# Chunk attention and two feed-forward layers on one core: tile 8's queries and keys in the later tiles' buffer, the last weights loaded in step 0, two buffers for transposed probabilities

## The chip, the cores and the metric

The kernel runs on one core of a Trainium2 chip. The metric is the device time of one execution in microseconds (us), the median over several executions.

## The reference

Queries, keys and values have 8 batches, 8 heads, 576 positions and 64 columns each. Attention is done within chunks of 64 positions; its result, laid out as 4608 tokens by 512 columns, goes through two feed-forward layers (512 to 2048 to 512) with different activations:

```python
scores = scale * np.matmul(q_c, k_c.transpose(0, 1, 2, 4, 3))   # per chunk of 64
scores = scores - np.max(scores, axis=-1, keepdims=True)
attn = np.exp(scores)
attn = attn / (np.sum(attn, axis=-1, keepdims=True) + 1e-09)
out = np.matmul(attn, v_c)
x = out.transpose(0, 2, 1, 3).reshape(B * S, H * D)
h = x @ w_in1;  g = np.maximum(h, 0.0) + alpha * np.minimum(h, 0.0);  y = g @ w_out1
h = y @ w_in2;  g = h - np.tanh(h);  out = g @ w_out2
```

The four weight matrices arrive as 64-bit floats, read as 64-bit words.

## The kernel before, in words

The tokens are cut into 36 tiles of 128 and into 9 blocks of 512 (4 tiles). The kernel runs 18 passes, the plan: first layer one over the 9 blocks, then layer two. A pass has 16 steps, one for each block `f` of 128 of the 2048 inner columns. In a step TensorE makes the up product of block `f` (`up`, line 412, 12 matrix products into a PSUM buffer of which there are two) and the down product of the step two back (`down`, line 471, 12 products); between them ScalarE and VectorE compute the activation (`act_g`, line 426) and split it into a high and a low half (`split_g`, line 449). Every factor is split that way, so each product is three.

A weight block of layer one is loaded as 64-bit words (`load_w`, line 135), turned to 32-bit floats by ScalarE and VectorE (`convert_a`, lines 107 and 108; `convert_b`, lines 118 to 128) and split by ScalarE (line 153) and GpSimd (line 154). This happens in the first pass, beside its 16 steps: `(f, 0)` is the up weight of block `f`, `(f, 1)` the down weight. Each has a memory slot of its own, `w{which}_{f}`, and some slots are used earlier for something else: 12 and 13 for the queries and keys of tiles 4 to 7, 14 and 15 for those of tiles 0 to 3, `(15, 0)` once more for those of tile 8. The list `LATE` (line 517) says in which step the loads of blocks 10 to 15 are placed.

The attention of tiles 0 to 3 is a prologue. That of tile `t` from 4 on is spread over steps of the passes, from its `base[t]` (line 535: 3, 5, 7, 9 for tiles 4 to 7, 12 for tile 8, then every 4 steps). Its parts are the transposes of queries and keys (`att_a_natural`, line 243, on TensorE; `att_a`, line 267, on VectorE at line 272 for tiles loaded in pieces), the scores (`att_s`, line 278, step base), the softmax (`att_e`, `att_n`, base + 1 and + 2), the transpose of the probabilities and its copies into `ptb` (`att_t`, `att_d`, lines 337, 346 and 347, base + 3), the product with the values (`att_v`, line 349, base + 4, and + 5 for tile 7) and the splitting of the result into the block's input (`att_x`, lines 400 and 404, one step on). Transposes on TensorE, scores and value products use one PSUM buffer, `ps_a`. Where a tile's value product falls in the step of another tile's scores, `beside` lets it use the second part of that tile's buffer.

From tile 9 on the queries and keys of one to two tiles (a unit) are loaded in at least 32 small transfers into a buffer of which there is one, `raw` (`begin_unit`, line 213, `some_loads`, line 232). A unit may begin at the step `free`, and its transfers are spread over the steps up to three before its scores. Tiles with `t % 9 == 4` are loaded whole into the same buffer (`load_natural_late`).

All of this is written in the order of the steps; a planner of the framework then orders each engine's queue by its own times, save in the prologue, which is kept as written. Loads and stores are all issued by SyncE. The lines that decide here:

```python
beside[t] = next((u for u in base if base[u] == pv), None)          # line 574
both = banks.get(beside.get(t)) or new_banks("xp")                  # line 352
turn = {4: 2, 5: 2, 6: 6, 7: 6, 8: 10}                              # line 546
at(r, some_loads, -(-32 // max(1, last - free)))                    # line 558
```

Of the kernel before, what the change touches and what calls it, by code (L numbers as in the profile page):

```python
# [9 lines left out]
F32 = mybir.dt.float32  # L10
# [17 lines left out]
def kernel(  # L28
# [23 lines left out]
    P = 128  # L52
    HP = H // 2
# [5 lines left out]
    const = ctx.enter_context(tc.tile_pool(name="const", bufs=1))  # L59
# [16 lines left out]
    zero = const.tile([P, P], F32, name="zero")  # L76
    bias_sb = const.tile([P, 1], F32, name="bias_sb")
    ktc = const.tile([P, 2, HP, 2, D], F32, name="ktc")
    ptb = const.tile([P, 2, HP, 2, 32], F32, name="ptb")


    wsplit = {}
# [1 line left out]
    def slot(f, which, shape, dtype):  # L84
        return wpool.tile(shape, dtype, tag=f"w{which}_{f}", name=f"w{which}_{f}")
# [91 lines left out]
    raws, qts, kts, vts, ps, pts, xps = {}, {}, {}, {}, {}, {}, {}  # L177
# [22 lines left out]
    def load_natural(t, raw):  # L200
        for i in range(2):
            natural_into(raw[:, i], t, i)
        raws[t] = raw[:, 0], raw[:, 1]

    def load_natural_early(t, f):
        load_natural(t, slot(f[0], f[1], [P, 2, H * D], F32))

    def load_natural_late(t):
        load_natural(t, rawp.tile([P, 2, H * D], F32, tag="raw", name="rawn"))
# [29 lines left out]
    def new_banks(name):  # L239

        return ps_a.tile([P, 2, 512], F32, tag="a", name=name)
# [34 lines left out]
    scs, banks, beside = {}, {}, {}  # L276
# [62 lines left out]

    def att_d(t):  # L340

        pt, pn = pts.pop(t), ptb.rearrange("p e h a i -> p (e h) a i")
        for c in range(2):
            for a in range(2):
                o, i = 64 * c + 32 * a, 64 * c + 32 * (1 - a)
                nc.vector.tensor_copy(pn[o:o + 32, :, 1 - a, :], pt[i:i + 32, :, a, :])
                nc.scalar.activation(out=pn[o:o + 32, :, a, :], in_=pt[o:o + 32, :, a, :], func=AF.Copy)

    def att_v(t):

        vt = vts.pop(t)
        both = banks.get(beside.get(t)) or new_banks("xp")
        xp = both[:, :, HP * D:].rearrange("p c (h d) -> p c h d", h=HP)
        for hp in range(HP):
            for e in range(2):
                for c in range(2):
                    r = slice(64 * c, 64 * c + 64)
                    nc.tensor.matmul(
                        out=xp[64 * e:64 * e + 64, c, hp, :],
                        lhsT=vt[r, 2 * hp + e],  # L360
                        rhs=ptb[r, e, hp].rearrange("p a i -> p (a i)"),
                        start=True,
                        stop=True,
                    )
        xps[t] = xp
# [140 lines left out]
    def split_y(j, kk, x):  # L506
# [7 lines left out]
    NPT = NB // P  # L514
    LAG = 2
    SCRATCH = 10
    LATE = [(0, (10, 0)), (0, (10, 1)), (0, (11, 0)), (0, (11, 1)), (0, (14, 0)), (0, (14, 1)), (3, (13, 0)), (3, (13, 1)), (7, (12, 0)), (7, (12, 1)),
            (12, (15, 0)), (12, (15, 1))]

    events = {}  # L520

    def at(step, fn, *args, first=False):
        todo = events.setdefault(max(step, 0), ([], []))
        todo[0 if first else 1].append((fn, args))
# [8 lines left out]
    base = {}  # L533
# [13 lines left out]
    free = 0  # L547
    for unit in units:
        t = unit[0]
        if t % 9 == 4 and t > 9:  # L550
            turn[t] = base[t] - 1
            at(free, load_natural_late, t)
            free = turn[t] + 1
        elif t >= 9:
            last = base[t] - 3
            at(free, begin_unit, t, len(unit))
            for r in range(free, last + 1):
                at(r, some_loads, -(-32 // max(1, last - free)))
            for i, tt in enumerate(unit):
                at(base[t] - 2 + i, att_a, tt)  # L560
            free = base[t] + len(unit) - 2
        else:
            free = 8
        for t in unit:
            s = base[t]
            at(s, att_s, t)
            at(s + 1, att_e, t, first=True)
            at(s + 2, att_n, t)
            at(s + 3, att_t, t, first=True)
            at(s + 3, att_d, t, first=True)  # L570
    for t in range(NPT, NT // P):
        pv = base[t] + (5 if t == 7 else 4)
        if t != 7:
            beside[t] = next((u for u in base if base[u] == pv), None)
        at(pv - 2, load_v, t)
        at(pv, att_v, t)
        at(pv + 1, lambda t: att_x(t, get_x(t // NPT), t % NPT * P), t)
    for t in turn:
        at(turn[t], att_a_natural, t)
    for step, piece in LATE:  # L580
        at(step, load_w, *piece)
# [24 lines left out]
    with tc.manual_schedule():  # L606
        make_identity(nc, ident)
        nc.vector.memset(zero, 0.0)
        nc.vector.memset(bias_sb, TS[1])
        kt = rawp.tile([P, 4, HP, 2, D], F32, tag="raw", name="kt")  # L610
        for t in range(4):
            if t % 2 == 0:
                qt = slot(10, t // 2, [P, 2, HP, 2, D], F32)
            qts[t], kts[t] = qt[:, t % 2], kt[:, t]
        load_natural_early(0, (15, 0))
        load_natural_early(1, (15, 1))
        load_w(0, 0)
        load_natural_early(2, (14, 0))
        load_natural_early(3, (14, 1))
        load_v(0)  # L620
        load_v(1)
        load_w(1, 0)
        load_v(2, (11, 0))
        load_v(3, (11, 1))
        arow = stage.tile([P, 512], F32, tag="st", name="arow")
        nc.sync.dma_start(out=arow[:KF, :P], in_=alpha.rearrange("(f p) -> f p", p=P))
        load_w(2, 0)
        load_w(0, 1)
        load_w(3, 0)
        load_natural_early(4, (13, 0))  # L630
        load_w(1, 1)
        load_w(4, 0)
        load_natural_early(5, (13, 1))
        load_w(2, 1)
        load_w(5, 0)
        load_natural_early(6, (12, 0))
        load_w(3, 1)
        load_natural_early(7, (12, 1))
        for f in range(4, 10):
            if f > 5:  # L640
                load_w(f, 0)
            load_w(f, 1)

        def warm(n, to=None):
            for _ in range(n):
                nc.tensor.matmul(out=dummy if to is None else to, lhsT=zero, rhs=zero, start=True, stop=True)

        dummy = ps_y.tile([P, P], F32, tag="y3", name="dummy")
        first_banks = new_banks("first")
        x0 = get_x(0)  # L650
        scratch.extend(xpool.tile([P, 4, 512], F32, tag=f"x{w}", name=f"scr{w}") for w in "hl")
        warm(7)
        att_a_early(0, 0)
        warm(1)
        att_a_early(0, 1)
        warm(1)
        att_a_early(1, 0)
        att_s_early(0)
        att_a_early(1, 1)
        att_e(0, True)  # L660
        warm(3)
        att_s_early(1)
        att_n(0)
        convert_a((0, 0))
        att_a_early(2, 0)
        att_e(1, True)
        warm(4)
        att_a_early(2, 1)
        convert_b((0, 0), ops=(0, 1))
        att_t_early(0)  # L670
        warm(2)
        att_s_early(2)
        att_n(1)
        convert_b((0, 0), ops=(2,))
        att_a_early(3, 0)
        att_a_early(3, 1)
        att_e(2, True)
        convert_b((0, 0), ops=(3,))
        warm(3)
        att_s_early(3)  # L680
        att_t_early(1)
        att_n(2)
        split_w(0, 0, nc.gpsimd)
        warm(1)
        att_v_early(0)
        att_e(3, True)
        att_t_early(2)
        att_xh(0, x0, 0)
        att_v_early(1)
        convert_a((1, 0))  # L690
        att_n(3, nc.vector)
        att_xl(0, x0, 0)
        more = first_banks[:, 0, 0:P]
        warm(2, more)
        att_xh(1, x0, P)
        att_v_early(2)
        last_a = att_t_early(3)
        att_xl(1, x0, P)
        convert_b((1, 0), ops=(0, 1))
        att_xh(2, x0, 2 * P)  # L700
        att_xl(2, x0, 2 * P)
        att_v_early(3)
        convert_b((1, 0), ops=(2, 3))
        split_w(1, 0, nc.gpsimd)
        hp0 = up(0, x0, NB, slice(0, 2 * P))
        att_x(3, x0, 3 * P)
        at_ps = first_banks[:, 0, 0:KF]
        nc.tensor.transpose(at_ps, arow[:KF, :P], ident[:KF, :KF])
        nc.scalar.activation(out=alpha_sb, in_=at_ps, func=AF.Copy)
        nc.scalar.activation(out=nalpha_sb, in_=at_ps, func=AF.Copy, scale=-1.0)  # L710
        load_natural_early(8, (15, 0))

    queue, late = [], []

# [9 lines left out]
    for j, (layer, t0) in enumerate(plan):  # L724
        x = get_x(j)
        acc = []
        for f in range(KF):
            hp = up(0, x0, NB, slice(2 * P, NB), hp0) if j == f == 0 else up(f, x, NB)
# [53 lines left out]
```

## Time and profile before

| | |
|---|---|
| median of 3 runs (lowest to highest) | 1731.82 us (1729.38 to 1732.12) |
| the profiled execution | 1729.36 us |
| its span in the profile | 1727.6 us |
| TensorE busy, products | 1670.8 us (97%) |
| VectorE, ScalarE, GpSimd busy | 1324.7, 689.5, 352.3 us |
| the first pass over the weights, about | 45 to 181 us of the span |
| layer one after it, about | 181 to 906 us |
| layer two, about | 906 us to the end |

Times are counted from the start of the span. PE is TensorE (PEld its weight loads), DVE VectorE, ACT ScalarE, POOL GpSimd, SPq SyncE's queue. A row of a timeline gives the start, the duration, the engine, the line of the kernel, the operation, what it writes and reads, how many instructions the row merges, and in brackets the idle time before it with what ended it. The granted clock is the share of TensorE's full speed that the chip granted.

### The profile page before, as it was taken

Reading aid. Unit: us, or ns where it says so; the run is one execution under the profiler, and the core shown is the slowest. Engines: PE = TensorE matmul, PEld = TensorE weight load, DVE = VectorE, ACT = ScalarE, POOL = GpSimd, SP = SyncE. Lnnn points to the kernel's source line nnn. Section 1 sums busy time; section 2 is a strip of 40 time slices with the busy share of each in tenths; the row PEclk is TensorE's granted clock in tenths of the full one; section 3 lists DMA queues with packets and bytes.
Section 4 is the critical chain, followed back from the end, with each engine's and each line's share of the span. In section 5 each row is a group of like instructions: output and inputs, shape, how many; then the busy total and the mean of one; then the engine's idle time right before and its main releaser. Section 6 shows DMA issues by size and latency. Waiting matters only on the chain.

```text
span 1727.6 us, 24773 instructions
## 1 busy us (share of the span) xinstructions
PE 1670.8 (97%) x9389; PEld 1360.8 (79%) x9389; DVE 1324.7 (77%) x2163; ACT 689.5 (40%) x1304; POOL 352.3 (20%) x264
## 2 busy tenths in 40 slices
PE   8877999999999999999999999999999999999998
PEld 7665788788887888888888778888888888888886
DVE  7988866778667868684437797978787878888776
ACT  6665422333322424231334444435353434344433
POOL 3663100000000000000243222222222222222221
PEclk9988999999999999999999999999999999999999
DMA  9811404433153514320422010101010101000000
GB/s 245 253 55 43 133 13 105 116 86 98 50 111 67 156 28 135 57 92 1 146 74 74 1 49 1 49 1 49 1 49 1 49 1 49 1 25 1 25 1 25
DMA packets 215591, 108.58 MB, mean 63 GB/s; under 512 B 170912, under 2 KB 187312, under 8 KB 215472
## 3 DMA queue, kind: packets, MB, share of 16 engines
q1 hardware_dynamic: 215472, 107.01, 22.8%
q8 instruction: 73, 1.20, 0.3%
q14 instruction: 46, 0.38, 0.1%
HBM read 79.70 MB, written 27.26 MB: 62 GB/s over the span
## 4 chain that ended last, share of the span: by engine, by line
PE 51%; DVE 21%; ACT 8%; issue 5%; SPq 3%; DMA 3%; POOL 0%; ACTq 0%; DVEq 0%; POOLq 0%
PE y L478 25%; PE hps L420 24%; DVE g L467 4%; DVE g L469 4%; DVE g L468 4%; DVE g L465 3%; SPq L232 3%; ACT ghi L450 2%; ACT sq L460 2%; DVE ktc L464 2%; ACT w L462 2%; DMA rw<-in_moe_w_in_dram 1%; DVE xl L509 1%; ACT th L461 1%; PE sc L287 1%
## 5 line engine op out<-in xcount | busy, mean ns | idle before, releaser
L420 PE MATMUL hps<-xh,w 128*128 128x512 f32 (+1 forms) x2312 | 589.1, 395 | 18.7 <-DVE g L444 6.2
L420 PEld LDWEIGHTS hps<-xh,w 128*128 128x128 f32 x2312 | 431.1, 189 | 118.2 <-DVE g L444 9.5
L450 ACT ACTIVATE ghi<-g 128x512 fp32r<-128x512 f32 x288 | 181.9, 632 | 721.9 <-DVE g L469 447.6
L451 POOL TENSOR_TENSOR glo<-g,ghi 128x512 fp32r<-128x512 f32 x159 | 218.2, 1372 | 610.4 <-ACT ghi L450 576.7
L420 PE MATMUL hps<-xl,w 128*128 128x512 f32 (+1 forms) x1156 | 311.6, 391 | 0.0
L478 PE MATMUL y<-w,ghi 128*128 128x512 f32 x1152 | 294.2, 393 | 8.2 <-ACT ghi L450 3.7
L478 PE MATMUL y<-ghi,w 128*128 128x512 f32 x1152 | 289.9, 392 | 3.2 <-ACT ghi L450 3.2
L478 PEld LDWEIGHTS y<-w,ghi 128*128 128x128 f32 x1152 | 215.1, 189 | 60.1 <-ACT ghi L450 8.6
L478 PEld LDWEIGHTS y<-ghi,w 128*128 128x128 f32 x1152 | 216.9, 189 | 49.7 <-ACT ghi L450 4.1
L420 PEld LDWEIGHTS hps<-xl,w 128*128 128x128 f32 x1156 | 218.1, 189 | 45.6
L464 DVE TENSOR_SCALAR ktc<-sq 128x512 uint32<-128x512 f32 x144 | 136.3, 947 | 135.0 <-ACT sq L460 135.0
L441 DVE TENSOR_SCALAR g<-hps,alpha_sb 128x512 f32<-128x512 f32 x128 | 95.4, 746 | 93.4 <-PE hps L420 90.8
L332 POOL TENSOR_TENSOR p<-p,rd 128x512 f32<-128x512 f32 x35 | 39.0, 1113 | 618.3 <-DVE rd L331 568.3
L478 PE MATMUL y<-w,glo 128*128 128x512 f32 x576 | 159.1, 389 | 0.0
L478 PE MATMUL y<-glo,w 128*128 128x512 f32 x576 | 157.3, 392 | 0.2 <-POOL glo L451 0.2
L451 DVE TENSOR_TENSOR glo<-g,ghi 128x512 fp32r<-128x512 f32 x129 | 97.3, 754 | 68.8 <-ACT ghi L450 68.5
L478 PEld LDWEIGHTS y<-glo,w 128*128 128x128 f32 x576 | 108.4, 189 | 23.1 <-POOL glo L451 0.6
L478 PEld LDWEIGHTS y<-w,glo 128*128 128x128 f32 x576 | 108.3, 188 | 22.8
L469 DVE COPY_PREDICATED g<-ktc,th 128x512 f32<-128x512 uint32 x144 | 122.9, 853 | 4.4
L467 DVE SCALAR_TENSOR_TENSOR g<-w,g 128x512 f32<-128x512 f32 x144 | 106.6, 741 | 0.0
L462 ACT ACTIVATE w<-sq,bias_sb 128x512 f32<-128x512 f32 x144 | 104.5, 726 | 0.0
L468 DVE SCALAR_TENSOR_TENSOR g<-sq,g 128x512 f32<-128x512 f32 x144 | 100.6, 699 | 4.7
(101 smaller groups left out, 1475.4 us busy)
## 6 DMA issues: line engine op xcount, KB each, us to landing
ysc<-yst SPq DMA_DIRECT2D x36, 256.0 KB, 2.5
yraw<-ysc SPq DMA_DIRECT2D x9, 1024.0 KB, 5.5
out_dram<-yst SPq DMA_DIRECT2D x36, 256.0 KB, 2.5
w<-in_moe_w_in_dram SPq DMA_DIRECT2D x16, 512.0 KB, 6.1
w<-in_moe_w_out_dram SPq DMA_DIRECT2D x16, 512.0 KB, 6.3
rw<-in_moe_w_in_dram SPq DMA_DIRECT2D x32, 256.0 KB, 3.2
rw<-in_moe_w_out_dram SPq DMA_DIRECT2D x32, 256.0 KB, 3.2
w<-wm SPq DMA_DIRECT2D x32, 256.0 KB, 2.1
```

The costliest lines, as they stand in the source:

```text
L232: nc.sync.dma_start(out=o, in_=i)
L420: nc.tensor.matmul(out=hp[:, cols], lhsT=w[:, a, m], rhs=x[b][:, kk, cols], start=(kk == 0 and i == 0), stop=(kk == KD - 1 and i == 2),)
L441: nc.vector.tensor_scalar(out=g, in0=hp, scalar1=0.0, scalar2=alpha_sb[:, f:f + 1], op0=ALU.min, op1=ALU.mult)
L450: nc.scalar.activation(out=hi, in_=g, func=AF.Copy)
L451: lo_engine.tensor_tensor(out=lo, in0=g, in1=hi.bitcast(F32), op=ALU.subtract)
L462: nc.scalar.activation(out=w, in_=sq, func=AF.Square, bias=bias_sb)
L464: nc.vector.tensor_scalar(out=mask, in0=sq, scalar1=0.375 ** 2, scalar2=None, op0=ALU.is_ge)
L465: nc.vector.scalar_tensor_tensor(out=g, in0=sq, scalar=cc, in1=hp, op0=ALU.mult, op1=ALU.mult)
L467: nc.vector.scalar_tensor_tensor(out=g, in0=w, scalar=ce, in1=g, op0=ALU.add, op1=ALU.mult)
L468: nc.vector.scalar_tensor_tensor(out=g, in0=sq, scalar=ca, in1=g, op0=ALU.add, op1=ALU.mult)
L469: nc.vector.copy_predicated(g, mask, th)
L478: nc.tensor.matmul(out=acc[t], lhsT=lhsT, rhs=rhs, start=(f == 0 and i == 0), stop=(f == KF - 1 and i == 2))
```

## The change

Tile 8's queries and keys are loaded into `raw`, the buffer of the later tiles, in place of the slot of weight block 15; block 15's two loads move from step 12 to step 0. The units that use `raw` after it may begin at step 11 in place of 8, so that the 32 transfers of tiles 9 and 10 are placed 16 to a step in steps 11 and 12 in place of 7 to a step from step 8. The value product of tile 6 moves from step 11 to step 12, where tile 8's scores are, and uses their PSUM buffer; its values' load and its splitting move by a step with it. `ptb` has two halves, used in turn by even and odd tiles.

```diff
-    ptb = const.tile([P, 2, HP, 2, 32], F32, name="ptb")
+    ptb = const.tile([P, 2, 2, HP, 2, 32], F32, name="ptb")
...
-        pt, pn = pts.pop(t), ptb.rearrange("p e h a i -> p (e h) a i")
+        pt, pn = pts.pop(t), ptb[:, t % 2].rearrange("p e h a i -> p (e h) a i")
...
-                        rhs=ptb[r, e, hp].rearrange("p a i -> p (a i)"),
+                        rhs=ptb[r, t % 2, e, hp].rearrange("p a i -> p (a i)"),
...
-    LATE = [(0, (10, 0)), (0, (10, 1)), (0, (11, 0)), (0, (11, 1)), (0, (14, 0)), (0, (14, 1)), (3, (13, 0)), (3, (13, 1)), (7, (12, 0)), (7, (12, 1)),
-            (12, (15, 0)), (12, (15, 1))]
+    LATE = [(0, (10, 0)), (0, (10, 1)), (0, (11, 0)), (0, (11, 1)), (0, (14, 0)), (0, (14, 1)), (0, (15, 0)), (0, (15, 1)),
+            (3, (13, 0)), (3, (13, 1)), (7, (12, 0)), (7, (12, 1))]
...
-            free = 8
+            free = 11
...
-        pv = base[t] + (5 if t == 7 else 4)
-        if t != 7:
-            beside[t] = next((u for u in base if base[u] == pv), None)
+        pv = base[t] + (5 if 6 <= t <= 7 else 4)
+        beside[t] = next((u for u in base if base[u] == pv), None)
...
-        load_natural_early(8, (15, 0))
+        load_natural_late(8)
```

## Rows read from the trace of the kernel before

**Rows 1.** The page: busy us (share of the span) and instructions of each engine.

```profile
PE 1670.8 (97%) x9389; PEld 1360.8 (79%) x9389; DVE 1324.7 (77%) x2163; ACT 689.5 (40%) x1304; POOL 352.3 (20%) x264
```

**Rows 2.** Busy time by stretch, columns as in the first line.

```profile
core 0: us, PE busy (x) PEld busy (x) DVE busy (x) ACT busy (x) POOL busy (x), PEclk, DMA share, GB/s
...
60.00:130.00 70.00, 55.23 (x296) 41.74 (x295) 65.25 (x91) 46.04 (x85) 45.51 (x27) 0.88 0.41 108
...
143.80:158.70 14.90, 4.02 (x74) 3.06 (x73) 9.77 (x21) 8.59 (x18) 1.04 (x1) 0.65 0.20 54
158.70:173.00 14.30, 13.75 (x81) 10.51 (x82) 14.19 (x21) 7.98 (x15) 9.39 (x7) 0.89 0.28 45
173.00:906.00 733.00, 726.22 (x4788) 593.00 (x4787) 507.26 (x1004) 231.69 (x471) 64.29 (x54) 1.00 0.33 86
906.00:1728.00 822.00, 807.98 (x3527) 659.48 (x3525) 665.80 (x923) 352.18 (x637) 201.10 (x150) 1.00 0.07 24
```

**Rows 3.** Timeline of TensorE from 135 to 175 us.

```profile
135.92 1.98 PE L420 MATMUL hps<-xh,w 128*128 128x512 f32 x8
...
142.74 1.07 PE L478 MATMUL y<-glo,w 128*128 128x512 f32 x4
147.36 0.63 PE L251 MATMUL tr<-ident,w 128*128 128x128 f32 x4 [3.55 <-issue]
148.78 1.11 PE L251 MATMUL tr<-ident,w 128*128 128x128 f32 x4 [0.79 <-DVE qt L253]
150.58 1.13 PE L358 MATMUL xp<-ptb,v 64*64 64x64 f32 x32 [0.69 <-ACT ktc L255]
154.97 1.13 PE L287 MATMUL sc<-ktc,qt 64*64 64x64 f32 x32 [3.27 <-DVE xl L404]
158.69 3.53 PE L420 MATMUL hps<-xh,w 128*128 128x512 f32 x8 [2.59 <-ACT w L153]
...
174.84 0.69 PE L287 MATMUL sc<-ktc,qt 64*64 64x64 f32 x32
```

**Rows 4.** Timeline of VectorE and ScalarE from 146 to 159 us.

```profile
146.58 0.68 DVE L404 TENSOR_TENSOR xl<-sc,xh 128x512 fp32r<-128x512 f32 x1
...
149.93 0.60 ACT L255 ACTIVATE ktc<-tr 128x512 f32<-128x512 f32 x1 [3.50 <-PE tr L251]
...
151.81 1.69 ACT L347 ACTIVATE ptb<-pt 32x256 f32<-32x256 f32 x4 [1.28 <-PE xp L358]
...
154.13 0.67 ACT L107 ACTIVATE wm<-w 128x512 f32<-128x512 f32 x1
...
156.39 0.59 ACT L435 ACTIVATE neg<-hps 128x512 f32<-128x512 f32 x1
...
156.87 0.60 ACT L436 ACTIVATE g<-hps 128x512 f32<-128x512 f32 x1
...
158.01 0.63 ACT L153 ACTIVATE w<-wm 128x512 fp32r<-128x512 f32 x1
```

**Rows 5.** Timeline of SyncE's queue.

```profile
69.69 7.12 SPq L232 DMA_DIRECT2D raw<-in_q_dram  x13
...
149.92 0.37 SPq L91 DMA_DIRECT2D w<-in_moe_w_in_dram  x1
...
162.45 7.74 SPq L232 DMA_DIRECT2D raw<-in_q_dram  x16
```

**Rows 6.** DMA view of 38 to 66 us: packets and bytes.

```profile
DMA packets 10479, 9.40 MB, mean 336 GB/s; under 512 B 6254, under 2 KB 9326, under 8 KB 10477
```

**Rows 7.** DMA issues from 162 to 181 us; the last column is us to landing (median).

```profile
raw<-in_k_dram SPq DMA_DIRECT2D x16, 32.0 KB, 2.1
```

**Rows 8.** Waits of VectorE over the span: us in total, times, longest.

```profile
DVE ktc L272 <- DMA raw<-in_k_dram: 14.4, 7, 5.4
```

**Rows 9.** Timeline of VectorE and GpSimd at 126 and 154 us.

```profile
126.50 1.73 POOL L451 TENSOR_TENSOR glo<-g,ghi 128x512 fp32r<-128x512 f32 x1
...
127.01 1.50 DVE L118 TENSOR_SCALAR wm<-wm 128x512 f32<-128x512 f32 x1
...
154.82 0.43 DVE L118 TENSOR_SCALAR wm<-wm 128x512 f32<-128x512 f32 x1
```

## The prediction

> **What bounds the kernel now.** I read the page's busy shares first, then the busy time by stretch, then the timeline of one stretch. TensorE is busy for nearly the whole span [rows 1], so only time in which it stands still, or runs at its lower clock, can be won. By stretch [rows 2] there is little of that in most places: from 173 to 906 us TensorE is busy 726.2 of 733 us, from 906 us to the end 808.0 of 822. The losses lie in the first block of 512 tokens. From 60 to 130 us it is busy 55.2 of 70 us while VectorE is busy 65.3 of 70: there the VectorE bounds, with the conversion of weights, and the change takes no instruction out of that. The stretch from 143.8 to 158.7 us is another matter: TensorE works 4.0 of 14.9 us, its granted clock is 0.65, VectorE has 5.1 us idle and ScalarE 6.3.
>
> The timeline of TensorE shows what stands in this hole [rows 3]: the last product before it ends at 143.81 us, then come the transposes of tile 8 in two halves, the value product of tile 6 at 150.58, the scores of tile 8 at 154.97, and at 158.69 the up product of weight block 15. The other engines' rows [rows 4] say why each is late. The transposes wait for the low half of tile 5's result (146.58 + 0.68 = 147.26 us), since all of these share one PSUM buffer. The keys of tile 8 are copied out at 149.93 + 0.60 = 150.53. The product of tile 6 then takes the buffer for itself, and the scores get it only when ScalarE and VectorE have read that product: 150.58 to 154.97, 4.4 us. Meanwhile SyncE's load of weight block 15, which reuses the memory of tile 8's queries and keys, is issued at 149.92 us, right after the transposes have read it [rows 5]. ScalarE starts a conversion at 154.13, and only behind the conversions in its queue come the two readings of a finished up product at 156.39 to 157.47; the split at 158.01 releases TensorE. So three things end together near 158.6: the late weights, the late reading of the product's buffer, and the PSUM handoff.
>
> **The change part by part.** *Weights of block 15 at step 0, tile 8 in the later tiles' buffer.* The wait of the load for the transposes goes: its issue at 149.92 is no longer on the path. What is late next is ScalarE. After the keys' copy at 150.53 its queue still holds the four copies of tile 7's probabilities, 1.69 us, and the two readings, 1.08 us (156.39 to 157.47) [rows 4]: 150.53 + 1.69 + 1.08 = 153.3 us, with the conversion of block 15 done in ScalarE's and VectorE's earlier gaps. The up product then starts at about 153.4 in place of 158.69: 5.3 us won. The ends of this term: if only the conversion moves and the readings stay behind, nothing is won (0); if the whole hole closes, 14.9 - 4.0 = 10.9 us, and as the first eight products after the hole took 3.53 us where eight took 1.98 at 135.92 [rows 3], up to 1.55 more: 12.4. I take 5.3, since the transposes' own wait (until 147.26) and ScalarE's queue stay. The clock was 0.65 in the hole, between the two levels of 1.2 and 2.4 GHz, and 1.00 in the stretches after 173 us [rows 2]; in a hole of some 9.6 us I expect the same low clock and count none of the 1.55.
>
> *Tile 6's product one step later, in the buffer of tile 8's scores.* One handoff of the PSUM buffer falls away, the 4.4 us above. It runs beside the wait of the up product, so it is inside the 5.3 and not added; were it not done, the scores would stand in TensorE's queue until 154.97 and hold back the up product behind them, and 158.69 - 154.97 - 1.13 = 2.6 us would be the most the weights alone could give.
>
> *Two buffers for the transposed probabilities.* The moved product needs them: tile 7's copies come in the step in which tile 6's product is now made. In the trace they waited for that product once, ScalarE until 151.81 by 1.28 us [rows 4]. No instruction is added. From the second block on the copies come three steps after the product that reads them, and nothing waits: 0.
>
> *Two loads of 512 KB more at step 0.* At 38 to 66 us the DMA engines move 9.40 MB at 336 GB/s [rows 6]; 1 MB more takes 1.05 / 336 GB/s = 3.1 us there. Behind them in SyncE's queue stand the values of tiles 4 and 5 and the loads of blocks 12 and 13. The 32 transfers of tiles 9 and 10, 1 MB too, which the trace has there before 70 us [rows 5], leave the same place, so I take 0, with ends 0 and 3.1.
>
> *The loads of tiles 9 and 10 from step 11.* They now wait until tile 8's transposes have read the buffer, 149.9 us. Sixteen took 162.45 to 170.19 us to issue, 0.484 each [rows 5]; 32 take 15.5, and the last lands 2.1 us later [rows 7]: 167.5 us. Two VectorE transposes for tile 9, two for tile 10, then the scores of tile 9 at about 169. In the trace those scores come at 174.84 [rows 3]; 5.3 us earlier is 169.5. So they are just in time: 0, but with no slack left. The load of tiles 11 and 12, before at 162.45, moves to about 170, ends near 187, and its tile is not due before step 24, so that has cover, unless VectorE reaches its transposes early. Their price, if late: VectorE stands behind the transpose, and the activations behind it in its queue hold TensorE. The longest such wait in the trace is 5.4 us [rows 8]. Ends: 0 and two such waits, 10.8.
>
> Sum: -5.3. The profiled execution took 1729.36 us, 2.5 below the median of 1731.82; the difference is put on the median: 1726.5 us.
>
> **The rivals.** *The whole hole closes.* If the order on ScalarE changes too, so that the readings of the finished product go ahead of the keys' copy, TensorE can run up products in place of standing: -12.4, 1719.4 us. For it: the product they read was ready before the hole, since no up product stands in it [rows 3]. Against: the transposes' wait and the 4 us of attention work remain.
>
> *VectorE sets the end anyway.* After the hole VectorE is busy 14.19 of 14.30 us [rows 2]; the conversion of block 15 would move to a time when GpSimd works. A conversion pass that took 0.43 us at 154.82, with GpSimd idle, took 1.50 at 127.01, beside GpSimd's 1.73 us subtraction at 126.50 [rows 9]. Two such passes for each of two parts, 1.07 us more each: 4.3 us. Then 5.3 - 4.3 = 1.0 is won: 1730.8 us, no change. The decision is where in VectorE's queue these passes fall. The Trainium skill, GPSIMD Engine Reference, section "1. Specifications", says that GpSimd's SBUF interfaces are shared with VectorE and that VectorE instructions in a two-port mode, or with two SBUF inputs, contend for them; the trace agrees (0.43 against 1.50), and by that rule the early place of the conversion is the worse one.
>
> *The loads of tiles 9 to 12 come too late (slower).* They are issued one behind the other from 149.9 us. If the transposes of tile 9, which VectorE had at the head of its queue long before, or of tile 11 stand there before the data, VectorE waits as it did 5.4 us in the worst case, twice: -5.3 + 10.8 = +5.5, 1737.3 us. It decides from the point where VectorE reaches them over 2.6 us early in each of two places. For it: there are seven waits on such keys, 14.4 us in all [rows 8]. Against: in the stretch that holds them TensorE lost 733 - 726.2 = 6.8 us altogether [rows 2].
>
> **How the numbers follow.** The forecast has a chance of 0.47, the closed hole 0.15, VectorE 0.21, the late loads 0.17. About 0.2% or 3.5 us is what a measurement of this kernel can tell from no change. Of the forecast's 0.47 I put 0.05 on a gain under 3.5 us. So faster 0.42 + 0.15 = 0.57, same 0.05 + 0.21 = 0.26, slower 0.17. The range goes from the closed hole, 1719, to just short of the late loads' full price, 1736; the forecast's own range is 1722 to 1730.
>
> **What would show it.** In the profile after, the hole between the down product of block 12 and the up product of block 15 is some 9.6 us long, with the scores of tile 8 and the product of tile 6 back to back right after the keys' copy; the load of block 15 stands among those of step 0; ScalarE's split of block 15 comes before its reading of the last free product; the 32 transfers of tiles 9 and 10 begin at tile 8's transposes. VectorE passes of 1.5 us in block 15's conversion would show the second rival, VectorE waits for keys of tiles 9 or 11 of several us the third. The prediction is wrong if the hole stays 15 us, if it is closed but its gain is lost between 160 and 220 us, or if the stretches before 130 us or after 220 change by over 2 us.

## The result, and the profile after

The kernel after the change takes 1740.01 us (median of four runs, 1737.07 to 1741.18); four runs of the kernel before gave 1731.22 (1729.38 to 1732.12). The ratio is 1.0051, with a 95% interval of 1.0038 to 1.0064: slower, by 8.8 us, where 1726.5 had been forecast and 1736 was the upper end of the range. The profiled execution took 1740.66 us with a span of 1738.9; before, 1729.36 and 1727.6.

The page's busy times after, beside [rows 1], show no added instruction: the counts are the same. VectorE is busy 8.7 us longer with the same 2163.

```profile
PE 1675.5 (96%) x9389; PEld 1364.3 (78%) x9389; DVE 1333.4 (77%) x2163; ACT 689.0 (40%) x1304; POOL 347.6 (20%) x264
```

Busy time by stretch after (the columns are those of [rows 2]):

```profile
130.00:143.80 13.80, 8.36 (x40) 5.47 (x42) 13.73 (x21) 8.23 (x16) 6.07 (x6) 0.98 0.00 1
143.80:158.70 14.90, 11.29 (x101) 8.84 (x97) 14.43 (x20) 7.04 (x15) 8.17 (x6) 0.84 0.08 19
158.70:173.00 14.30, 8.68 (x103) 7.17 (x107) 10.20 (x19) 6.99 (x14) 3.89 (x3) 0.74 0.20 41
173.00:181.00 8.00, 6.42 (x49) 4.88 (x42) 3.73 (x8) 2.25 (x5) 1.04 (x1) 0.72 0.41 67
181.00:200.00 19.00, 15.01 (x118) 12.01 (x117) 12.82 (x24) 4.64 (x9) 1.05 (x1) 0.91 0.53 122
```

and three of these stretches before:

```profile
130.00:143.80 13.80, 12.94 (x115) 10.17 (x113) 12.33 (x23) 5.32 (x12) 5.20 (x4) 1.00 0.10 22
173.00:181.00 8.00, 7.50 (x91) 5.89 (x90) 6.22 (x11) 3.42 (x7) 2.04 (x2) 1.00 0.47 85
181.00:200.00 19.00, 19.00 (x144) 15.59 (x143) 16.98 (x44) 10.34 (x24) 1.04 (x1) 1.00 0.61 195
```

In the stretch of the hole TensorE now works 11.29 of the 14.9 us, where it worked 4.02 before [rows 2]. In part the hole only moved: ahead of it TensorE works 8.36 of 13.80 us (12.94 before), and behind it 8.68 of 14.30 (13.75 before), 6.42 of 8.00 (7.50) and 15.01 of 19.00 (19.00). TensorE's timeline after shows what moved, beside [rows 3]:

```profile
143.60 1.13 PE L287 MATMUL sc<-ktc,qt 64*64 64x64 f32 x32 [4.86 <-DVE sm L330]
...
148.03 2.00 PE L420 MATMUL hps<-xh,w 128*128 128x512 f32 x8
...
160.01 1.09 PE L251 MATMUL tr<-ident,rawn 128*128 128x128 f32 x4 [4.74 <-issue]
...
165.69 1.07 PE L478 MATMUL y<-glo,w 128*128 128x512 f32 x4
166.60 0.60 PE L251 MATMUL tr<-ident,rawn 128*128 128x128 f32 x4
167.89 0.69 PE L287 MATMUL sc<-ktc,qt 64*64 64x64 f32 x32 [0.69 <-ACT ktc L255]
...
172.67 1.13 PE L358 MATMUL xp<-ptb,v 64*64 64x64 f32 x32 [3.62 <-issue]
174.51 5.28 PE L420 MATMUL hps<-xh,w 128*128 128x512 f32 x16 [0.71 <-ACT xh L400]
180.67 2.12 PE L420 MATMUL hps<-xl,w 128*128 128x512 f32 x8 [0.88 <-DVE xl L404]
186.08 0.69 PE L287 MATMUL sc<-ktc,qt 64*64 64x64 f32 x32 [3.30 <-DVE ktc L272]
...
187.94 3.58 PE L420 MATMUL hps<-xh,w 128*128 128x512 f32 x8 [0.70 <-DVE g L444]
```

The last up product of the first block starts at 148.03 in place of 158.69, and the block's last down product ends at 166.76; before, it ended at 180.89. But the transposes of tile 8 come at 160.01 and 166.60 in place of 147.36 and 148.78, its scores at 167.89 in place of 154.97, the value product of tile 7 at 172.67 in place of 163.70, the next block's first up products at 174.51 in place of 167.32, and the scores of tile 9 at 186.08 in place of 174.84.

Put as an account: by 167.2 us the first block and the transposes are done. What the kernel before had done by 180.9 us and the kernel after still had to do is the scores of tile 8 (with tile 6's product beside them in the kernel after), tile 7's product, 24 up products of the next block and the scores of tile 9 with the product beside them: at the distances of full clock (8 products in 1.82 us, from 180.72 to 182.54 before) about 1.1 + 0.6 + 5.5 + 1.2 = 8.4 us. So by this estimate the kernel after stood 180.9 - 167.2 - 8.4 = 5.3 us ahead, as much as forecast. It had finished this list at 187.24, not at 175.6: 11.6 us lost, 6.3 net, and some 2.5 more until 200 us, where eight up products still take 3.58 us. The loss then stays: the second block's store is issued at 285.47 before and at 294.31 after, 8.8 us later.

VectorE's timeline after says why tile 8's transposes are late:

```profile
146.19 1.40 DVE L122 TENSOR_SCALAR wm<-wm 128x512 int32<-128x512 int32 x1
147.63 1.42 DVE L124 SCALAR_TENSOR_TENSOR wm<-w,wm 128x512 int32<-128x512 int32 x1
149.18 1.56 DVE L128 CUSTOM_DVE_ANT_0 wm<-wm,wr 128x1024 uint16<-128x1024 uint16 x1
...
154.21 1.40 DVE L118 TENSOR_SCALAR wm<-wm 128x512 f32<-128x512 f32 x1
...
155.99 0.68 DVE L316 TENSOR_REDUCE mx<-sc 128x8 f32<-128x512 f32 x1
...
159.23 0.68 DVE L404 TENSOR_TENSOR xl<-sc,xh 128x512 fp32r<-128x512 f32 x1
```

and the same softmax in the kernel before (its low half `xl`, at 146.58, stands in [rows 4]):

```profile
143.81 0.69 DVE L316 TENSOR_REDUCE mx<-sc 128x8 f32<-128x512 f32 x1
```

In the kernel before, the maximum of the scores of tile 7 is taken 4.8 us after their product began (138.98). After, it is taken 12.4 us after it (143.60 to 155.99). VectorE isn't idle: passes of weight conversion stand ahead of it in its queue. The last four conversions of the first pass over the weights (by the order in which the kernel writes them both parts of block 15 and the down parts of blocks 13 and 14) begin with their passes of line 118 at 136.26, 138.03, 145.75 and 154.21 us; in the kernel before, where block 15's load was issued at 149.92, at 154.82, 155.97, 159.71 and 165.55. So not only block 15's passes moved ahead, but also those that had stood beside and behind them. Of the delay, 4.6 us have arisen before tile 7's scores begin (138.98 before, 143.60 after), in the softmax of tile 6. The low half that frees the shared PSUM buffer, which the transposes wait for, moves from 146.58 to 159.23, by 12.65 us; the transposes by the same. VectorE's later rows show the second place:

```profile
176.80 0.71 DVE L272 STREAM_TRANSPOSE qt<-raw 128x512 f32<-128x512 f32 x1 [3.91 <-DMA raw<-in_q_dram]
...
185.22 1.31 DVE L272 STREAM_TRANSPOSE ktc<-raw 128x512 f32<-128x512 f32 x2 [4.61 <-DMA raw<-in_k_dram]
186.45 0.71 DVE L441 TENSOR_SCALAR g<-hps,alpha_sb 128x512 f32<-128x512 f32 x1
```

SyncE's queue after, beside [rows 5]:

```profile
167.23 8.02 SPq L232 DMA_DIRECT2D raw<-in_q_dram  x16
175.29 7.84 SPq L232 DMA_DIRECT2D raw<-in_k_dram  x16
```

The loads of tiles 9 and 10 can't start before tile 8's transposes have read the buffer, and those end at 167.2; so they run from 167.23 to 183.13, and VectorE waits for them twice, 3.91 and 4.61 us, with the activation of a finished up product right behind (186.45), for which TensorE waits at 187.94.

### The profile page after: what moved, and what is told of

Its sections match the earlier page's. It is cut to its first block, busy times and chain, and to the rows that moved or that the text cites. A ratio compares the mean times of both kernels' runs of the same rounds, so it can differ in the third digit from the quotient of the medians.

```text
span 1738.9 us, 24758 instructions
## 1 busy us (share of the span) xinstructions
PE 1675.5 (96%) x9389; PEld 1364.3 (78%) x9389; DVE 1333.4 (77%) x2163; ACT 689.0 (40%) x1304; POOL 347.6 (20%) x264
## 4 chain that ended last, share of the span: by engine, by line
PE 51%; DVE 25%; ACT 7%; issue 7%; SPq 6%; DMA 4%; ACTq 0%; DVEq 0%
PE y L478 25%; PE hps L420 24%; SPq L232 5%; DVE g L467 3%; DVE g L469 3%; DVE g L468 3%; DVE g L465 3%; ACT ghi L450 2%; ACT sq L460 2%; DVE ktc L464 2%; DMA rw<-in_moe_w_in_dram 1%; ACT w L462 1%; DVE xl L509 1%; DVE wm L124 1%; ACT th L461 1%
## 5 line engine op out<-in xcount | busy, mean ns | idle before, releaser
L420 PEld LDWEIGHTS hps<-xh,w 128*128 128x128 f32 x2312 | 432.9, 190 | 114.0 <-DVE g L444 10.8
```

The costliest lines, as they stand in the source:

```text
L420: nc.tensor.matmul(out=hp[:, cols], lhsT=w[:, a, m], rhs=x[b][:, kk, cols], start=(kk == 0 and i == 0), stop=(kk == KD - 1 and i == 2),)
```

## The experiments

Two theories stood against each other. **Theory 1**: the loss is the order on VectorE, the early conversions ahead of tile 7's softmax. **Theory 2**: it is the loads of tiles 9 and 10, tied to tile 8's buffer. The medians of the kernel before were 1729.61 us (experiments 1 to 4), 1731.26 (5 to 8) and 1730.66 (9 to 12); ratios are to these. Diffs are against the kernel after unless said otherwise; `issue_after` puts the instructions inside it behind the named one in their engine's queue; the lists that keep the named instructions are left out of the diffs.

**1. Hold block 15's conversion back.** The passes on VectorE come after the low half of tile 5's result (the one at 159.23 above). The down weight of block 13 is converted in the same call as the up weight of block 15 and is held with it.

```diff
-            nc.vector.tensor_tensor(out=to, in0=xp, in1=hi.bitcast(F32), op=ALU.subtract)
+            xl_ins[t] = nc.vector.tensor_tensor(out=to, in0=xp, in1=hi.bitcast(F32), op=ALU.subtract)
...
-        to_f32_b([w_parts[piece] for piece in pieces], ops)
+        with tc.issue_after(xl_ins[5].ins) if pieces[0][0] == 15 else nullcontext():
+            to_f32_b([w_parts[piece] for piece in pieces], ops)
```

> The changed kernel, with VectorE's part of the last conversions (blocks 15 and the down weight of 13) put behind the low half of tile 5's result in VectorE's queue; tile 8 still in the later tiles' buffer. Theory 1 (order): the loss comes from these conversions, which no longer wait for a load and so stand ahead of the softmax of tiles 6 and 7 in VectorE's queue; tile 8's transposes came 12.7 us later for it (160.0 against 147.4). Then they return to 150 or before, the scores of tile 9 to 176 or before, and the time is 1727 to 1732 us. Theory 2 (late loads): the loss comes from the 32 loads of tiles 9 and 10, which wait for tile 8's transposes whatever the order; then VectorE still waits 4 us and more for them twice, TensorE stands before the scores of tile 9, and the time is 1736 to 1740 us.

Measured: 1736.82 us, 1.0038 [1.0023, 1.0053]. The transposes are back at 150.89 and 153.88, and the second block's store comes at 289.93, 4.4 us earlier than after the change. By the time alone the gain is not clear of noise (the interval of the change was 1.0038 to 1.0064); the two stores and experiments 9 and 10 say that the order is a part of the loss. It is not all of it: the time lies where Theory 2 had it, so Theory 1 alone falls. Yet Theory 2's sign is missing, too: VectorE waits 0.73 us for the keys of tiles 9 and 10, and not twice 4.

**2. A buffer of its own for tile 8.** The loads of tiles 9 and 10 go back to step 8's place.

```diff
-        load_natural_late(8)
+        load_natural(8, const.tile([P, 2, H * D], F32, name="raw8"))
...
-            free = 11
+            free = 8
```

> The changed kernel, with tile 8's queries and keys in a buffer of their own (4 KB per partition more), so that the loads of tiles 9 and 10 may begin at step 8 as before. Theory 1 (order): tile 8's transposes stay at about 160 us, the block's last input at about 174; only the 3.3 us wait of TensorE and VectorE's two waits go: 1734 to 1738 us. Theory 2 (late loads): VectorE no longer waits for these tiles, and the time falls below the kernel before: 1725 to 1731 us.

Measured: 1745.02 us, 1.0079 [1.0056, 1.0103], above what either theory gave and not below the change itself. TensorE's timeline:

```profile
159.92 1.09 PE L251 MATMUL tr<-ident,raw 128*128 128x128 f32 x4 [3.34 <-issue]
...
175.65 1.13 PE L358 MATMUL xp<-ptb,v 64*64 64x64 f32 x32 [6.10 <-issue]
180.41 5.41 PE L420 MATMUL hps<-xh,w 128*128 128x512 f32 x16 [3.63 <-ACT xh L400]
```

and VectorE's:

```profile
169.15 1.30 DVE L272 STREAM_TRANSPOSE qt<-raw 128x512 f32<-128x512 f32 x2 [1.02 <-PE sc L287]
...
170.97 0.25 DVE L118 TENSOR_SCALAR wm<-wm 128x256 f32<-128x256 f32 x1
171.14 0.68 DVE L316 TENSOR_REDUCE mx<-sc 128x8 f32<-128x512 f32 x1
```

Without the wait for the loads, transposes from `raw` and passes over later blocks' weights stand ahead of tile 8's softmax, and tile 7's product is later still (175.65 against 172.67). Theory 2 alone falls, and what falls with it is the idea that the causes simply add up: here one wait was taken away, and other work whose data were early stood ahead.

**3. Both edits, 1 and 2.**

> Both edits at once: the conversions held behind tile 5's result and tile 8 in a buffer of its own. Theory 1 and theory 2 together: the gain that was forecast for the change comes out, 1723 to 1728 us. If it stays at 1731 or above, there is a third cause, VectorE's own load in this stretch. If it equals the run with the held conversions, the late loads cost nothing; if it equals the run with the buffer of its own, the order costs nothing.

Measured: 1735.16 us, 1.0029 [1.0014, 1.0044], the range of a third cause. Until the scores of tile 9 it is ahead of the kernel before: 24 up products and those scores are done at 178.8 us. Then VectorE and TensorE show

```profile
183.43 0.71 DVE L272 STREAM_TRANSPOSE ktc<-raw 128x512 f32<-128x512 f32 x1 [4.82 <-PE y L478]
```

```profile
187.67 2.79 PE L420 MATMUL hps<-xh,w 128*128 128x512 f32 x8 [3.40 <-DVE g L444]
```

A transpose of tile 11's keys, whose load was issued until 181.6 us, holds VectorE; the activations wait behind it, and TensorE for them, 3.40 us. The gain is lost at waits of a kind that the kernel before has too [rows 8].

**4. Tile 8 in the slot of weights (15, 1), those weights loaded at step 12.**

```diff
-        load_natural_late(8)
+        load_natural_early(8, (15, 1))
...
-            free = 11
+            free = 8
...
-    LATE = [... (0, (15, 0)), (0, (15, 1)), ... (7, (12, 0)), (7, (12, 1))]
+    LATE = [... (0, (15, 0)), ... (7, (12, 0)), (7, (12, 1)), (12, (15, 1))]
```

> The changed kernel, with tile 8's queries and keys in the slot of the down weight of block 15 in place of the later tiles' buffer: the loads of tiles 9 and 10 may begin at step 8 as before, and only the down weight of block 15 waits for tile 8's transposes. Theory 1 (order): one of the two early conversions, the up weight's, stays ahead of the softmax; half of the delay of tile 8's transposes goes, 1730 to 1735 us. Theory 2 (late loads): VectorE's waits for tiles 9 and 10 are gone, 1725 to 1731 us, as with the buffer of its own.

Measured: 1742.3 us, 1.0071 [1.0055, 1.0086], which neither theory gave. Tile 8's transposes stand at 159.22 and 163.36, so with half of the early weights they are as late. Behind them TensorE stands 8.62 us, until 174.84, for the split of the weights that are loaded late, which adds a wait that the change doesn't have.

**5. Experiment 3, and VectorE's transposes held.** From tile 11 on they come behind the latest activation written before them.

```diff
-            nc.vector.scalar_tensor_tensor(out=g, in0=hp, scalar=0.0, in1=g, op0=ALU.max, op1=ALU.add)
+            gs.append(nc.vector.scalar_tensor_tensor(out=g, in0=hp, scalar=0.0, in1=g, op0=ALU.max, op1=ALU.add))
...
+    def att_a_held(t):
+        with tc.issue_after(gs[-1].ins) if gs else nullcontext():
+            att_a(t)
...
-                at(base[t] - 2 + i, att_a, tt)
+                at(base[t] - 2 + i, att_a_held, tt)
```

> The run with both edits, and in addition every VectorE transpose of queries and keys from tile 11 on is put behind the activation of the step it is written in, in VectorE's queue. Theory 3 (head of the queue): with both edits the first block ended 2 us ahead of the kernel before, and the gain was lost at 178 to 190 us, where VectorE stood 4.8 us before tile 11's keys and the activation behind it held TensorE 3.4 us and took its clock down. Then VectorE does not stand there, and the time falls by 3 to 5 us to 1729 to 1732. Rival (parked weights): the activation is held by the conversion of the second layer's weights, whose loads come late, and the time stays at 1733 to 1736 us.

Measured: 1728.73 us, 0.9985 [0.9974, 0.9996]: 6.4 us less than experiment 3, a little more than Theory 3 of the expectation gave. TensorE still stands 2.74 us before its product at 187.69, since now a pass over a parked weight, a weight of layer two that is converted in the later blocks, stands at the head of VectorE's queue:

```profile
185.68 0.29 DVE L118 TENSOR_SCALAR wm<-wm 128x256 f32<-128x256 f32 x1 [5.07 <-ACT wm L107]
```

**6. Tile 6's product alone.** The kernel before, with the two halves of `ptb` and the moved product, without the loads.

```diff
-    ptb = const.tile([P, 2, HP, 2, 32], F32, name="ptb")
+    ptb = const.tile([P, 2, 2, HP, 2, 32], F32, name="ptb")
...
-        pv = base[t] + (5 if t == 7 else 4)
-        if t != 7:
-            beside[t] = next((u for u in base if base[u] == pv), None)
+        pv = base[t] + (5 if 6 <= t <= 7 else 4)
+        beside[t] = next((u for u in base if base[u] == pv), None)
```

> The kernel before with the third part of the change alone: two halves of the buffer for transposed probabilities, and tile 6's value product one step later in the buffer of tile 8's scores; tile 8's queries and keys and the weights of block 15 as in the kernel before. The prediction gave this part at most 2.6 us of gain. Theory 1 (order of the conversions) expects no loss from it: 1726 to 1731 us. If it is slower than 1733 us, the moved product itself delays the first block's end, and the order of the conversions is not the whole cause.

Measured: 1732.64 us, 1.001 [1.000, 1.002]: no gain. TensorE's timeline:

```profile
151.02 1.13 PE L287 MATMUL sc<-ktc,qt 64*64 64x64 f32 x32 [0.97 <-ACT ktc L255]
...
160.77 1.13 PE L358 MATMUL xp<-ptb,v 64*64 64x64 f32 x32 [7.77 <-issue]
162.29 2.07 PE L420 MATMUL hps<-xh,w 128*128 128x512 f32 x4 [0.39 <-ACT w L153]
```

The handoff is gone (the scores at 151.02 in place of 154.97), but now tile 7's product stands next in TensorE's queue, and it starts only at 160.77; the up product of block 15 comes behind it, at 162.29 in place of 158.69.

**7. The kernel before, with the transposes held** (the edit of 5, against the kernel before).

> The kernel before, with every VectorE transpose of queries and keys from tile 11 on put behind the activation of the step it is written in. Theory 3 (head of the queue): such transposes stood before their loads in the kernel before as well, 10 waits of 20 us together, and TensorE lost 6.2 us to activations in that stretch; part of it comes back, 1724 to 1728 us. Rival: the waits are covered by VectorE's slack, no change, 1728 to 1731 us.

Measured: 1725.51 us, 0.9970 [0.9961, 0.9979]: the hold is worth 5.7 us without the change, too.

**8. Experiment 5, and the conversions of the parked weights held as well** (those of the later blocks, on VectorE alone).

```diff
+    def park_held(*a):
+        with tc.issue_after(gs[-1].ins):
+            park_convert(*a)
...
-            at(s + h + 2, park_convert, f, which, h)
+            at(s + h + 2, park_held, f, which, h)
```

> As the run with both edits and held transposes, and the conversions of the second layer's parked weights (ScalarE's and VectorE's; only VectorE's part and what follows it can be held) behind the activation of their step too. If the parked weights hold the activations (rival of theory 3), this falls to 1724 to 1729 us while the run before it stays at 1733 to 1736. If theory 3 holds, both come out alike, 1729 to 1732 us.

Measured: 1718.77 us, 0.9933 [0.9918, 0.9948], below what either side of the expectation gave: both holds count.

With these holds little is lost in the later blocks (in 8, TensorE stands for 1.06 of 50 us from 300 to 350 and not at all from 350 to 700), so the parts of the change can be taken one by one. **9** is the change as it is, with all three holds (edits 1, 5 and 8). **10** is the change with edits 5 and 8 only, the early conversions left free. **11** is the kernel before with edits 5 and 8 only.

> The change as it is, tile 8 in the later tiles' buffer and step 11 for the loads of tiles 9 and 10, with all three orders held: the last conversions behind tile 5's result, the transposes from tile 9 on and the parked weights' conversions behind the activation of their step. It differs from the best run so far (1718.8 us) only by the late loads of tiles 9 and 10. Theory: with the orders held those cost 1 to 3 us, 1719 to 1723 us, well below the kernel before; so the change's parts are sound and VectorE's queue order made it slower. Rival (late loads): the loads of these tiles cost 5 us or more once nothing else does, 1724 to 1732 us.

> The change with the transposes from tile 9 on and the parked weights' conversions held, but the last weights' conversions free, as the change has them. Against the run before it, it gives what the early conversions cost by themselves: theory 1 (order) 4 to 8 us more, 1724 to 1730 us; if it comes out alike, the early conversions cost nothing and the loss was all in the transposes and parked weights.

> The kernel before with the same two holds, transposes and parked weights, and nothing of the change. If the change is worth something on this footing, this is slower than the best run so far: theory, by 2 to 5 us, 1721 to 1724 us (the best run was 2 us ahead at the first block's end). If it is as fast, 1718 to 1720, the change gives nothing in any order and the holds do it all.

Measured: 1723.3 us (9), 0.9958 [0.9945, 0.9972]; 1728.15 (10), 0.9985 [0.9976, 0.9994]; 1718.7 (11), 0.9929 [0.9914, 0.9944]. The first transposes of tile 8 and the scores of tile 9 on TensorE, for 10:

```profile
160.02 1.09 PE L251 MATMUL tr<-ident,rawn 128*128 128x128 f32 x4 [4.27 <-issue]
...
186.99 0.69 PE L287 MATMUL sc<-ktc,qt 64*64 64x64 f32 x32 [2.32 <-DVE ktc L272]
```

for 9:

```profile
150.32 1.09 PE L251 MATMUL tr<-ident,rawn 128*128 128x128 f32 x4 [6.07 <-issue]
...
181.19 0.69 PE L287 MATMUL sc<-ktc,qt 64*64 64x64 f32 x32
```

and for 8, the late loads gone too:

```profile
150.25 1.08 PE L251 MATMUL tr<-ident,raw 128*128 128x128 f32 x4 [6.84 <-issue]
...
176.21 0.69 PE L287 MATMUL sc<-ktc,qt 64*64 64x64 f32 x32
```

By these edits the sum is: 11 to 10, the change costs 1728.15 - 1718.70 = 9.45 us (8.8 without the holds). Of it the free conversions are 1728.15 - 1723.3 = 4.85 us (10 to 9), the moved loads of tiles 9 and 10 1723.3 - 1718.77 = 4.5 (9 to 8), and all the rest 0.07 (8 to 11): the earlier weights, kept in order, the moved product and the two halves win nothing that can be told from noise. The runs of 9 spread from 1721.75 to 1726.40 us, so each of the two large terms stands to some 2 us and their sum better; experiment 8 was timed beside runs of the kernel before with another median (1731.26 in place of 1730.66). The fourth combination, the conversions free and the loads in their old place, was not run with these holds; without them (experiment 2) it was no faster than the change. So the two terms hold for this order of taking the edits away.

The term of the moved loads is not time in which VectorE waits for them. In 9 they are issued from 154.46 us, and VectorE waits 0.68 us for the keys. What came late there is the last activation of the first block, on VectorE:

```profile
170.26 0.71 DVE L437 SCALAR_TENSOR_TENSOR g<-neg,nalpha_sb,g 128x512 f32<-128x512 f32 x1
...
172.86 1.31 DVE L272 STREAM_TRANSPOSE ktc<-raw 128x512 f32<-128x512 f32 x2 [0.68 <-DMA raw<-in_k_dram]
```

and on TensorE its down product:

```profile
172.77 3.78 PE L478 MATMUL y<-ghi,w 128*128 128x512 f32 x8 [2.80 <-ACT ghi L450]
```

In 8 the same activation stands ahead of the transpose of tile 8's probabilities, in 9 behind it, and behind ScalarE's copies of them (from 170.37 us) comes its split, at 172.09. The row of 8:

```profile
167.59 0.70 DVE L437 SCALAR_TENSOR_TENSOR g<-neg,nalpha_sb,g 128x512 f32<-128x512 f32 x1
```

So in 9, too, the delay that shows is one of order in VectorE's queue; whether a hold there would win the 4.5 us back was not tried. In 10 VectorE does wait for these loads (4.80 and 3.60 us), as after the change: there the loads are late because tile 8's transposes are, and this is part of the 4.85 us.

What the holds do to the kernel before shows in the windows of 11, the hole first:

```profile
143.80:158.70 14.90, 4.19 (x74) 2.85 (x72) 9.95 (x23) 8.76 (x18) 1.04 (x1) 0.69 0.20 54
...
300.00:350.00 50.00, 50.00 (x338) 40.87 (x337) 41.24 (x87) 18.95 (x40) 3.13 (x3) 1.00 0.41 89
```

The hole is still there; from 300 to 350 us TensorE doesn't pause, where the kernel before works 45.72 of the 50 us. Of TensorE's waits from 173 to 906 us the kernel before has

```profile
PE hps L420 <- DVE g L444: 6.2, 6, 2.9
```

(us in total, times, longest) and one wait of 0.4 us beside it; 11 has only the latter.

**12. Experiment 8, and the conversion of weights (14, 1) held too**, so that the hole might close further.

```diff
-        with tc.issue_after(xl_ins[5].ins) if pieces[0][0] == 15 else nullcontext():
+        with tc.issue_after(xl_ins[5].ins) if pieces[0] in ((15, 0), (14, 1), (15, 1)) else nullcontext():
```

> The best run so far with one more conversion, the down weight of block 14, behind tile 5's result. The hole before tile 8's transposes is still 6.8 us there, and VectorE makes that conversion in it. Theory: the transposes come 1 to 2 us earlier, and 0 to 2 us are won, 1717 to 1719 us. Rival: the down product of block 14 comes later for it, 1719 to 1722 us.

Measured: 1718.99 us, 0.9929 [0.9912, 0.9945], no gain over 8. Tile 8's transposes go to 147.24, tile 7's product to 168.94 (168.66 in 8): what is won ahead is lost behind. VectorE's busy time, the third of the columns:

```profile
140.00:160.00 20.00, 11.22 (x115) 8.54 (x105) 19.83 (x33) 11.01 (x22) 7.28 (x6) 0.70 0.12 27
```

It is full, 19.83 of 20 us (19.27 in 8). That the sum of VectorE's work sets the end of this stretch, whatever its order, is read from these two figures; it was not tried by taking work away.

The best versions are 11, 8 and 12, some 12 us below the kernel before and equal within their intervals; 11 is the simplest, since it has nothing of the change.

## Why the prediction was wrong

*The earlier weights, 5.3 us.* The first part of the step held: the load at 149.92 was off the path, the up product started 10.7 us earlier, and by the account above the first block stood 5.3 us ahead at its end. That this is the forecast's figure is luck, since the way to it was another: the forecast had the up product behind ScalarE's copy of tile 8's keys, at 153.4, and it came at 148.03, ahead of tile 8's transposes. The sentence that failed is the one behind the sum, that the transposes' own wait "(until 147.26)" stays. It was taken as fixed, while it hangs on the order of VectorE's queue, and that order is not the one of the trace before: the planner makes it anew. In the kernel before, the last four conversions stood behind tile 7's softmax (from 154.82 us on); with block 15's weights loaded in step 0 they stand ahead of it, and the transposes came 12.65 us later. Experiments 1 and 12 show it: with the conversions of block 15 and (13, 1) held the transposes are back at 150.89, and with (14, 1) held too at 147.24. The price of the free conversions, by experiments 10 and 9, is 4.85 us. The forecast's own list of signs had this outcome as one of being wrong: closed, but with its gain lost between 160 and 220 us.

*The loads of tiles 9 and 10, "just in time", 0 with an end of 10.8.* Failed as well, and first through the same step: they were dated from 149.9 us, where tile 8's transposes had been, and started at 167.23. The issue, 15.9 us for 32 (15.5 forecast), was right. With the transposes back (9) they start at 154.46 and are just in time, as forecast, with a wait of 0.68 us. Yet moving them still costs 4.5 us there, with the last activation behind other work in VectorE's queue: a term that the forecast doesn't have, and again one of order.

*Two loads of 512 KB more at step 0, 0.* Nothing speaks against it: by 100 us TensorE had made 127 of the first block's up products after the change and 132 before, by 130 us 178 and 168. One reading behind it was wrong: of the 32 transfers of tiles 9 and 10 the kernel before issued three ahead of 69.69 us, and the rest up to 86.68 us, not all before 70.

*Tile 6's product, inside the 5.3; the two halves of `ptb`, 0.* Right in result: 1.001 for both alone in experiment 6. The forecast said that without this part the weights would win 2.6 us at most; that was not tried.

*The rivals.* "VectorE sets the end anyway", at 0.21, named the right engine and the right question, where in VectorE's queue the passes fall. The rows show the price that it gave: the four passes quoted took 1.40, 1.42, 1.56 and 1.40 us, with GpSimd busy 8.17 us in the stretch (1.04 before [rows 2]), as here beside the third of them:

```profile
148.46 1.74 POOL L154 TENSOR_TENSOR w<-wm,w 128x512 fp32r<-128x512 f32 x1
```

Passes of the same lines between 154.82 and 157.93 in the kernel before took 0.43 (L118 and L122), 0.69 (L124) and 0.68 (L128). That is 0.97 + 0.73 + 0.88 + 0.97 = 3.55 us more, near the 4.3 forecast, though the rows don't say which of these passes are block 15's, and the kernel before has slow passes as well (1.33 and 1.66 us, at 169.86 and 171.23). The Trainium skill (GPSIMD Engine Reference, section "1. Specifications") states that VectorE's instructions in a two-port mode or with two SBUF inputs contend with GpSimd, whose SBUF interfaces are shared with VectorE; these rows agree. What the rival left out is that the attention of the next block stands behind these passes: it took the passes as an end of the gain, to 1730.8, and not as a delay of the chain that feeds the next block. How much of the 4.85 us is the slower passes and how much the order alone was not tried.

"The loads come too late", at 0.17, gave 1737.3, the nearest figure, and two waits of up to 5.4 us; the rows have 3.91 and 4.61. Its place was right and its start wrong by 17 us; that the figure came near is in part luck. That the whole hole closes (0.15) came nearest to what TensorE's window shows from 143.8 us on, but a part of the hole had moved ahead of that, and it was worth nothing. What happened has something of all three, and the cases had been priced as if only one could come true.

## What to carry to other kernels

Before an input is made available earlier, ask what the in-order queue that consumes it will do with it: work that is not urgent, once its data are early, can step ahead of a chain that is, and the date of everything behind has to be worked out anew, not read from the old trace. A hole in TensorE may be worth no more than the fullest other engine of that stretch can give: here VectorE went from 9.77 to 14.43 busy us of 14.9, and filling the hole was worth nothing; that the one follows from the other was not tried. Where an engine waits at the head of its queue for data that nobody needs yet, hold that work behind the urgent one: two such holds won 12 us in the kernel before, where no part of the change won any.

## What the runs showed that was not expected

The waits by which VectorE holds TensorE in the later blocks looked small: 6.2 us by the waits named for TensorE from 173 to 906 us, 6.8 by its idle time [rows 2]. Taking them away won 12.0 us by the medians (1730.66 to 1718.70) and 9.7 between the two profiled executions (1729.36 and 1719.68), and it is won in these blocks: the third block's store is issued at 374.58 before and 366.85 in experiment 11, the sixth's at 655.73 and 645.16. What the kernel before does from 173 to 906 us, 4788 instructions of TensorE in 733 us [rows 2], 11 does (4794 of them) in 723.3 us:

```profile
173.00:896.30 723.30, 722.76 (x4794) 593.31 (x4793) 516.80 (x1005) 234.08 (x471) 64.98 (x55) 1.00 0.34 88
```

Of these 9.7 us, 6.2 are idle time (6.8 before, 0.5 in 11) and 3.5 are busy time (726.22 and 722.76): products behind a wait run slower, and that counts as busy. At 331.21 before, behind a wait of 2.92 us, eight took 2.77 us, where eight took 1.98 at 135.92 [rows 3]. An engine's named waits were no upper bound for what their removal won.

Behind the new pauses of the kernel after the products ran slower. Sixteen up products at 174.51, behind pauses of 3.62 and 0.71 us, took 5.28 us with a granted clock of 0.72 in the stretch, between the levels of 1.2 and 2.4 GHz; sixteen at 167.32 before, in a run of products, took 3.96. The eight at 187.94 took 3.58, where eight at 195.03 took 1.98.
